# Asking for the first four weight tiles two at a time, and releasing the stores of projections two scores earlier, in an fp32 transformer block on one core

## The chip, the core and the metric

The kernel runs on one core of a Trainium2 chip. The metric is the device time of one execution in microseconds (us); lower is better. The times are medians of several runs. One further execution was recorded by the hardware profiler, and all rows of profiles come from such recorded executions.

The engines are named as in the profile: PE is TensorE (PEld its weight loads), DVE is VectorE, ACT is ScalarE, POOL is GpSimd, and SP is SyncE, which here does nothing but issue DMAs. Each engine works through its own queue in order.

## What is computed

One transformer block with adaptive layer norm on a sequence of 2048 rows of width 512, in float32, with 32 heads of width 16 and a hidden width of 1792:

```python
mod = (_silu(c) @ w_mod).reshape(c.shape[0], 6, 1, -1)
sa, ca, ga, sb, cb, gb = (mod[:, i] for i in range(6))
h = _layernorm(x) * (1 + ca) + sa
x = x + ga * attention(h, wqkv, wo)        # softmax over all 2048 keys, 32 heads
h = _layernorm(x) * (1 + cb) + sb
x = x + gb * (gelu(h @ w1 + b1) @ w2 + b2)
```

## The kernel before

**Precision.** Projections and the two feed-forward products are made of three products each: every operand is split into a high and a low part ("hi" and "lo", or the two halves of a `[P, 2, D]` tile), and high x high, low x high and high x low are added up in one PSUM bank. So each product of a 512-wide contraction is a group of 4 x 3 = 12 matmuls, and one over six hidden blocks of 128 a group of 18.

**Attention sets the pace.** There are 32 units, each with four heads and one batch of 512 queries (four batches `b`, eight units each). A unit has 16 steps, one for each 128 keys. A *half-step* (`half_step`, line 1007) is one such step; there are 512. It makes four *scores* (`exp_mm`, line 626: a matmul "e", then an exponential on ACT), four matmuls "mx" for the row maxima of a later unit (each reduced on DVE), and eight "pv" entries on PE in the profile, the four products of probabilities and values (`pv_step`). Scores and maxima use 64 of the 128 rows of the array, and so a matmul on the other 64 rows can run beside each of them.

**Background work** fills those other rows. `half_step` takes groups from the generator `jobs` (line 959, `work`) and issues up to `RUN` = 6 half-row matmuls of the current group in each half-step (`bg_mm`, line 985), on alternating halves of the rows; a group of 12 thus takes 24 half-row matmuls, four half-steps. When the generator gives `None`, the half-step has no background work and its scores and maxima run beside each other instead. When the two halves follow each other, line 996 makes the first matmul of the new half wait for an ACT instruction noted by `saw` after the last one. Background work is, in order:

- `block0` (line 930): the rest of the projections to queries, keys and values. A group for queries or keys ends in `evac` of `proj_qk` (line 305): ACT copies the bank, POOL makes the high and low part (lines 309, 310), and a store to DRAM is put off by `soon` (line 257). `soon(n, f)` emits `f` once n more scores have been emitted, and counts it in `owed` until then. `store_qk` (line 293) then puts two DMAs on SP.
- At its end, `block0` waits for all that is owed (line 952: no preparation, no owed store, no values and no division under way), closes the memory pools of the projections and opens that of the feed-forward part in the same place (`open_ffn`, line 680).
- For each batch b: `front(b)` (line 803), the output projection with `wo`, the second layer norm and its transposes; then `feed(b)` (line 857), the feed-forward part in three parts. `front` waits until the attention output of its batch is divided (`done[b]`, all four pieces of it), four scores more, and until its four tiles of `wo` have been asked for. `front(b + 1)` stands ahead of the last part of `feed(b)`. In the loop, GELU is done on ACT and POOL: the first half (lines 876 to 879) at the group's end, the second half (lines 882 to 887), which begins with a tanh, ten scores later.

The division (`o_prep`, line 702) reads the attention output of two units back from DRAM, inverts the denominators (14 scores later), stores them (2 later), loads them broadcast (5 later) and divides on POOL (7 later). At most two run at a time; the last one of a batch can begin eight scores after the batch's last unit has ended, and none of batch b begins before the hidden products of batch b - 1 are all emitted (`free_pc`, line 912).

**Weights of the later stages** are split once, kept in DRAM, and come back as tiles of 512 KB in a fixed order (`stream`, line 757: four tiles of `wo`, then those of w1 and w2). `wload` (line 769) asks for the next one if the pool is open and there is room: eight buffers, each free once the tile eight places before has been dropped. `wt` has every tile that was asked for so far, `used` every one that was dropped. Before the change `half_step` calls `wload` at the start of every odd half-step, and of an even one while fewer than `KC` = 4 tiles are waiting to be used.

**Order on the queues** is that of the program's text; there is no scheduler. SP runs ahead of the other engines and stops only where a DMA must wait for data or memory. `step_start` (line 1065) emits at the start of a half-step the loads that are due by then: queries (`qst`) and keys (`kh`) of the unit after next, and values (`vg`) of the next. The row maxima of a unit go through POOL (line 408) and DRAM into `qst` (line 419, "qst<-m") before its first score.

**The tail.** After 512 half-steps a group that is not finished is finished by itself, the last pv between its two halves of rows; then the remaining groups run on all 128 rows, then batch 3's output projection and feed-forward part.

Of the kernel before, what the change touches and what calls it, by code (L numbers as in the profile page):

```python
# [23 lines left out]
KC = D // P  # L24
# [45 lines left out]
def block_kernel(ctx: ExitStack, tc: tile.TileContext, x, wqkv, wo, w1, b1, w2, b2, c, w_mod, out):  # L70
# [88 lines left out]
    def stage(name):  # L159
        if first[0] and name in FIRST:  # L160
            return vpool.tile([P, D], F32, tag=name, name=name, bufs=FIRST[name])
        return spool.tile([P, D], F32, tag=name, name=name, bufs=STAGE[name])

    def pieces(name, dt=FR):
        return spool.tile([P, 2, D], dt, tag="parts", name=name, bufs=3)
# [83 lines left out]
    def later(n, f):  # L249
        if n:  # L250
            hooks.setdefault(clock["t"] + n, []).append(f)
        else:
            f()
# [3 lines left out]
    def soon(n, f):  # L257

        owed[0] += 1

        def g():
            owed[0] -= 1
            f()

        later(n, g)
# [27 lines left out]
    def store_qk(w, k, b, parts):  # L293
        stored.add((w, k, b))
        planes = qk_d[w][k].rearrange("i d o t -> (d o) i t")[:, :, b * TB : (b + 1) * TB]
        sy.dma_start(planes[:, 1 - w : 3 - w], parts.bitcast(F32))
        sy.dma_start(planes[:, 2 * w], parts[:, 0].bitcast(F32))

    def proj_terms(w, k, b):
        hi, lo = hT[b]  # L300
        t = wt_of[w, k]
        n = range(KC)
        return terms3([t[:, 0, i] for i in n], [t[:, 1, i] for i in n], [hi[:, i] for i in n], [lo[:, i] for i in n])

    def proj_qk(w, k, b):
        def evac(ps):
            parts, r = pieces("parts"), stage("pf")
            ac.activation(r, ps, AF.Copy)
            gp.tensor_copy(parts[:, 0], r)
            gp.tensor_tensor(parts[:, 1], r, parts[:, 0].bitcast(F32), op=ALU.subtract)  # L310
            soon(8, lambda: store_qk(w, k, b, parts))

        return proj_terms(w, k, b), "bg", evac

# [62 lines left out]
    def mx_mm(a):  # L377

        u, i = xorder[xc[a]] if xc[a] < 64 else divmod(xc[a], 32)
        xc[a] += 1  # L380
        kr, p, qc = i // 8, (i // 4) % 2, i % 4
        if u not in mxp:
            mxp[u] = small.tile([P, 16, 4], F32, tag="mxp", name="mxp")
            red[u] = 0
        ps = take("mx")
        r0 = a * 64
        te.matmul(ps, qst[u][r0 : r0 + KR, p, qc * P : (qc + 1) * P],  # L387
                  kh(u, kr // 2)[r0 : r0 + KR, p, (kr % 2) * TB : (kr % 2 + 1) * TB], start=True, stop=True)
        hc = (a * 2 + p) * 4 + qc

        def reduce():
            ins = ve.tensor_reduce(mxp[u][:, hc, kr : kr + 1], ps, axis=AX.X, op=ALU.max, negate=True)  # L392
            red[u] += 1
            if red[u] == 64:
                max_rows(u)
            return ins

        return reduce
# [227 lines left out]
    def exp_mm(a, bk="e"):  # L626

        s, p = divmod(ec[a], 2)
        while begun[0] < min(ec) // 2 + 1:
            begun[0] += 1  # L630
            step_start(begun[0] - 1)
        ec[a] += 1
        u, kc = divmod(s, NKC)
        assert u in mrows, (u, ec, xc, red, clock["t"])
        r0 = a * 64
        ps = take(bk)
        te.matmul(ps, kh(u, kc // 8)[r0 : r0 + KX, p, (kc % 8) * P : (kc % 8 + 1) * P], qst[u][r0 : r0 + KX, p],  # L637
                  start=True, stop=True)

        def act():  # L640
            t = ppool.tile([P, TB], F32, tag="p", name="p")
            saw(ac.activation(t, ps, AF.Exp, scale=SCALE))  # L642
            pt[4 * s + p * 2 + a] = t
            advance()

        return act
# [13 lines left out]
    def pv_step():  # L660
        s = cur["pv"]
        cur["pv"] += 1
        u, kc = divmod(s, NKC)
        if kc == 0:
            cur["ps"] = take("pv")
        for j in range(4):
            te.matmul(cur["ps"][32 * j : 32 * (j + 1)], vg[u][:, kc, j * VW : j * VW + 32], pt.pop(4 * s + j),  # L667
                      start=kc == 0, stop=kc == NKC - 1)
        if kc == NKC - 1:
            vg.pop(u)  # L670
            attn_out(u, cur["ps"])


    pools = {}
# [92 lines left out]
    wt, used, ringed, extra = {}, set(), [], []  # L767

    def wload():

        n = len(wt)
        if n == len(stream) or "f" not in pools:
            return
        key = stream[n]
        if extra:
            t = extra.pop()
        elif len(ringed) < WB or ringed[-WB] in used:
            t = pools["f"].tile([P, 2, D], FR, tag="w", name=f"w{key[1]}", bufs=WB)
            ringed.append(key)
        else:  # L780
            return
        sy.dma_start(t.bitcast(F32), {"o": wo_d, 1: w1_d, 2: w2_d}[key[1]][key[2]])
        wt[key] = t
# [201 lines left out]
    def bg_mm(h):  # L985

        g = act["g"]
        terms, bk, evac = g["group"]
        i = g["at"][h]
        if i == len(terms):  # L990
            return False
        if g["n"] == 0:
            g["ps"] = take(bk)
        ins = mm(g["ps"], terms[i], g["n"], 2 * len(terms), slice(h * 64, h * 64 + 64)).ins
        if g["n"] and g["half"] != h:
            tc.add_manual_dep(ins, g["seen"].name, AFTER, reason="both halves of the rows add to one bank")
        g["half"], g["seen"] = h, None
        g["at"][h] += 1
        g["n"] += 1
        if g["n"] == 2 * len(terms):  # L1000
            evac(g["ps"])
            act["g"] = None
        return act["g"] is not None
# [2 lines left out]

    def half_step(hs):
        h = hs % 2
        if h or len(wt) < len(used) + KC:
            wload()  # L1010
        if sides:
            sides.pop(0)()
        full = False
        if act["g"] is None:
            j = held.pop() if held else next(jobs, None)
            if callable(j):
                j()
                full = True
                j = next(jobs, None)
            if callable(j):  # L1020
                held.append(j)
            elif j is not None:
                act["g"] = {"group": j, "at": [0, 0], "n": 0, "seen": None}
        nx = min(64 * NU, LEAD + 4 * (hs + 1))
        ne = 4 * (hs + 1)

        def x_ok(a):
            return sum(xc) < nx and xc[a] < 32 * NU

        def e_ok(a):  # L1030
            return sum(ec) < ne and ec[a] < 2 * NU * NKC

        more = act["g"] is not None
        free = not more and not full
        k = 0
        while more and k < RUN:
            a = 1 - h
            more = bg_mm(h)
            if e_ok(a) and (sum(ec) < ne - 1 and k % 2 == 1 or not x_ok(a) and (sum(ec) < ne - 1 or k == RUN - 1)):
                exp_mm(a)()  # L1040
            elif x_ok(a):
                mx_mm(a)()
            k += 1
        while sum(ec) < ne or sum(xc) < nx:
            a = 0 if ec[0] <= ec[1] else 1
            fs = []
            if sum(ec) < ne:
                fs.append(exp_mm(a, "bg" if free and sum(ec) == ne - 1 else "e"))
                if x_ok(1 - a):
                    fs.append(mx_mm(1 - a))  # L1050
                elif e_ok(1 - a):
                    fs.append(exp_mm(1 - a))
            else:
                fs += [mx_mm(i) for i in range(2) if x_ok(i)]
            for f in fs:
                f()
        if hs:
            assert min(ec) >= 2 * cur["pv"] + 2
            pv_step()
# [24 lines left out]
    for hs in range(NU * NKC):  # L1084
        half_step(hs)
# [137 lines left out]
```

## Time and profile before

| | us |
|---|---|
| median of 3 runs | 1738.71 (1736.97 to 1739.3) |
| the profiled execution | 1738.16 |
| its span, from its first instruction to its last | 1736.3 |
| busy: PE, DVE, ACT, POOL | 1710.8, 1375.2, 1241.8, 685.0 |
| mean granted clock of TensorE | 0.997 |

In the profile's rows a DMA has the name of what it writes and what it reads (`wo<-wos`), and L782 is line 782 of the kernel. A row of the timeline or of the chain has the start in us, the length in us, the engine, and how many instructions of a kind were joined (x8). A row of waits names who waited for whom, the total in us, how often, and the longest. The stretches give for each of PE, PEld, DVE, ACT and POOL the busy time in us and the count of instructions, then the granted clock of TensorE, the share of the DMA engines, and GB/s.

### The profile page before, as it was taken

Reading aid. Unit: us, or ns where it says so; the run is one execution under the profiler, and the core shown is the slowest. Engines: PE = TensorE matmul, PEld = TensorE weight load, DVE = VectorE, ACT = ScalarE, POOL = GpSimd, SP = SyncE. Lnnn points to the kernel's source line nnn. Section 1 sums busy time; section 2 is a strip of 40 time slices with the busy share of each in tenths; the row PEclk is TensorE's granted clock in tenths of the full one; section 3 lists DMA queues with packets and bytes.
Section 4 is the critical chain, followed back from the end, with each engine's and each line's share of the span. In section 5 each row is a group of like instructions: output and inputs, shape, how many; then the busy total and the mean of one; then the engine's idle time right before and its main releaser. Section 6 shows DMA issues by size and latency. Waiting matters only on the chain.

```text
span 1736.3 us, 32537 instructions
## 1 busy us (share of the span) xinstructions
PE 1710.8 (99%) x12121; PEld 891.1 (51%) x12121; DVE 1375.2 (79%) x2298; ACT 1241.8 (72%) x2379; POOL 685.0 (39%) x688
## 2 busy tenths in 40 slices
PE   7999999999999999999999999999999999999999
PEld 6654444444444444444445444444445444444777
DVE  7998888888888888888889888888888888860332
ACT  3357778778777778778777778777877778778231
POOL 7333434435121256404631356404631356525310
PEclk8999999999999999999999999999999999999999
DMA  8646776767447534335454444335364344323554
GB/s 292 205 142 200 221 218 182 236 179 223 125 136 206 125 86 117 94 85 136 113 168 106 124 114 105 94 81 166 100 174 114 101 132 114 97 66 111 195 156 166
DMA packets 137130, 251.90 MB, mean 145 GB/s; under 512 B 25854, under 2 KB 45324, under 8 KB 136972
## 3 DMA queue, kind: packets, MB, share of 16 engines
q1 hardware_dynamic: 135712, 248.19, 50.3%
q8 instruction: 96, 1.57, 0.4%
q10 hardware_dynamic: 1260, 1.63, 0.3%
q14 instruction: 62, 0.51, 0.1%
HBM read 188.49 MB, written 61.28 MB: 144 GB/s over the span
## 4 chain that ended last, share of the span: by engine, by line
PE 91%; DVE 4%; ACT 2%; POOL 1%; DMA 1%; issue 1%; SPq 0%; ACTq 0%; POOLq 0%; DVEq 0%
PE bg L274 46%; PE pv L667 29%; PE e L637 11%; PE mx L387 3%; DVE mxp L392 2%; ACT p L642 1%; PE pr L274 1%; PE o L274 1%; PE warm L438 1%; DVE hTlo L481 1%; DVE bst L235 0%; ACT h L849 0%; DMA qst<-m 0%; PE mx L333 0%; PE bg L847 0%
## 5 line engine op out<-in xcount | busy, mean ns | idle before, releaser
L392 DVE TENSOR_REDUCE mxp<-mx 128x1 f32<-128x512 f32 x2048 | 1269.4, 682 | 201.4 <-PE mx L387 182.5
L642 ACT ACTIVATE p<-e 128x512 f32<-128x512 f32 x2032 | 1064.4, 605 | 308.1 <-PE e L637 292.8
L387 PE MATMUL mx<-kh,qst 48*128 48x512 f32 x2048 | 873.3, 441 | 1.9 <-DVE mxp L392 0.4
L637 PE MATMUL e<-qst,kh 50*128 50x512 f32 x2032 | 754.6, 419 | 7.0 <-ACT p L642 6.3
L667 PE MATMUL pv<-p,vg 128*32 128x512 f32 x4096 | 546.6, 605 | 0.0
L637 PEld LDWEIGHTS e<-qst,kh 50*128 50x128 f32 x2032 | 373.7, 186 | 148.7 <-ACT p L642 141.8
L387 PEld LDWEIGHTS mx<-kh,qst 48*128 48x128 f32 x2048 | 368.6, 185 | 21.1 <-DVE mxp L392 16.2
L274 PE MATMUL bg<-w,g 64*128 64x512 f32 (+1 forms) x1044 | 277.8, 404 | 0.0
L274 PEld LDWEIGHTS bg<-w,g 64*128 64x128 f32 (+1 forms) x1044 | 183.0, 185 | 142.7 <-ACT p L642 103.3
L274 PE MATMUL bg<-pchi,w 64*128 64x512 f32 (+1 forms) x656 | 194.5, 416 | 2.1 <-ACT p L642 2.0
L274 PEld LDWEIGHTS bg<-pchi,w 64*128 64x128 f32 (+1 forms) x656 | 109.0, 184 | 150.3 <-ACT p L642 102.2
L274 PE MATMUL bg<-hThi,wqkv 64*128 64x512 f32 x560 | 167.4, 418 | 0.3 <-ACT p L642 0.3
L274 PEld LDWEIGHTS bg<-hThi,wqkv 64*128 64x128 f32 x560 | 92.8, 184 | 118.9 <-ACT p L642 106.3
L667 PEld LDWEIGHTS pv<-p,vg 128*32 128x32 f32 x4096 | 81.4, 108 | 125.4 <-issue 117.6
L884 POOL TENSOR_SCALAR s<-s 128x512 f32<-128x512 f32 x40 | 59.8, 1496 | 137.4 <-ACT s L882 127.0
L903 POOL TENSOR_TENSOR x<-y,x 128x512 f32<-128x512 f32 x28 | 35.9, 1281 | 144.3 <-ACT y L902 139.3
L274 PE MATMUL bg<-pclo,w 64*128 64x512 f32 (+1 forms) x328 | 88.6, 389 | 0.0
L872 DVE TENSOR_TENSOR g<-h,g 128x512 fp32r<-128x512 f32 x16 | 11.6, 723 | 91.5 <-PE bg L274 62.7
L274 PE MATMUL bg<-hTlo,wqkv 64*128 64x512 f32 x280 | 76.4, 392 | 0.0
L819 POOL TENSOR_TENSOR x<-y,x 128x512 f32<-128x512 f32 x12 | 15.4, 1282 | 140.9 <-ACT y L816 114.8
L274 PEld LDWEIGHTS bg<-pclo,w 64*128 64x128 f32 (+1 forms) x328 | 60.5, 184 | 12.3
L274 PE MATMUL bg<-wo,pchi 64*128 64x512 f32 x192 | 64.8, 417 | 0.0
(160 smaller groups left out, 1331.9 us busy)
## 6 DMA issues: line engine op xcount, KB each, us to landing
kh<-qk SPq DMA_DIRECT2D x256, 192.0 KB
w<-w1s SPq DMA_DIRECT2D x56, 512.0 KB
w<-w2s SPq DMA_DIRECT2D x53, 512.0 KB
vg<-v SPq DMA_DIRECT2D x64, 332.0 KB
qk<-parts SPq DMA_DIRECT2D x32, 512.0 KB
qst<-qk SPq DMA_DIRECT2D x64, 192.0 KB
qk<-parts SPq DMA_DIRECT2D x32, 256.0 KB
ou<-osb SPq DMA_DIRECT2D x32, 256.0 KB
```

The source lines that it names most:

```text
L274: return te.matmul(ps, term[0][r], term[1][r], start=i == 0, stop=i == n - 1)
L387: te.matmul(ps, qst[u][r0 : r0 + KR, p, qc * P : (qc + 1) * P], kh(u, kr // 2)[r0 : r0 + KR, p, (kr % 2) * TB : (kr % 2 + 1) * TB], start= ...
L392: ins = ve.tensor_reduce(mxp[u][:, hc, kr : kr + 1], ps, axis=AX.X, op=ALU.max, negate=True)
L438: te.matmul(warm[:, :P], ident, ident, start=True, stop=True)
L481: e.tensor_tensor(hT[b][1][:, f], keep.pop(("H", b, f)), hT[b][0][:, f].bitcast(F32), op=ALU.subtract)
L637: te.matmul(ps, kh(u, kc // 8)[r0 : r0 + KX, p, (kc % 8) * P : (kc % 8 + 1) * P], qst[u][r0 : r0 + KX, p], start=True, stop=True)
L642: saw(ac.activation(t, ps, AF.Exp, scale=SCALE))
L667: te.matmul(cur["ps"][32 * j : 32 * (j + 1)], vg[u][:, kc, j * VW : j * VW + 32], pt.pop(4 * s + j), start=kc == 0, stop=kc == NKC - 1)
L819: gp.tensor_tensor(x2[t], y, x2[t], op=ALU.add)
L872: ve.tensor_tensor(g[:, 1], h, g[:, 0].bitcast(F32), op=ALU.subtract)
L884: gp.tensor_scalar(s, s, 1.0, None, op0=ALU.add)
L903: later(4, lambda: gp.tensor_tensor(x2[t], y, x2[t], op=ALU.add))
```

## The change

The store of a projection's parts is emitted six scores after the projection, not eight. And in a half-step, as long as the pool is open and fewer than four tiles have been asked for at all, `wload` is called twice; otherwise the old rule holds.

```diff
@@ -308,7 +308,7 @@
             ac.activation(r, ps, AF.Copy)
             gp.tensor_copy(parts[:, 0], r)
             gp.tensor_tensor(parts[:, 1], r, parts[:, 0].bitcast(F32), op=ALU.subtract)
-            soon(8, lambda: store_qk(w, k, b, parts))
+            soon(6, lambda: store_qk(w, k, b, parts))
 
         return proj_terms(w, k, b), "bg", evac
 
@@ -1006,7 +1006,7 @@
 
     def half_step(hs):
         h = hs % 2
-        if h or len(wt) < len(used) + KC:
+        for _ in range(2 if "f" in pools and len(wt) < KC else h or len(wt) < len(used) + KC):
             wload()
         if sides:
             sides.pop(0)()
```

## The prediction

> **What bounds the kernel now.** I read the page's shares first, then its chain, then the chain in order of time around the place that the change touches.
>
> ```profile
> span 1736.3 us, 32537 instructions
> PE 1710.8 (99%) x12121; PEld 891.1 (51%) x12121; DVE 1375.2 (79%) x2298; ACT 1241.8 (72%) x2379; POOL 685.0 (39%) x688
> PE 91%; DVE 4%; ACT 2%; POOL 1%; DMA 1%; issue 1%; SPq 0%; ACTq 0%; POOLq 0%; DVEq 0%
> ```
>
> TensorE (PE) is busy for 99% of the span and is 91% of the chain. So the change gains only where it puts PE work beside work that has to be done anyway, and loses wherever PE is made to stand. The profiled execution took 1738.16 us: span 1736.30 and 1.86 around it. It lies 0.55 us under the median of the runs, 1738.71.
>
> The chain around the first output projection shows the size of a half-step, which ends with eight "pv" matmuls:
>
> ```profile
> 518.98 1.00 PE pv L667 x8
> ...
> 521.88 1.00 PE pv L667 x8
> ...
> 530.11 1.00 PE pv L667 x8
> 531.10 0.42 PE e L637
> ...
> 538.32 1.00 PE pv L667 x8
> 539.32 0.45 PE bg L274
> ...
> 541.28 1.00 PE pv L667 x8
> ```
>
> From 518.98 to 521.88 is a half-step with background work (bg): 2.90 us; from 538.32 to 541.28 another, 2.96; I take 2.92. Between 521.88 and 538.32 there is no bg: 16.44 us are six idle half-steps of 2.74. I call them I1 to I6; I4 begins at 531.1, after the pv of 530.11. So a half-step's worth of bg, when it is put into an idle half-step, costs only 0.18 us there. Waiting for the four tiles of wo is part of these six.
>
> **What the change does, by the code's own clock.** A half-step is four scores. The last projection's copy (line 308) is emitted at the sixth bg matmul of its half-step, when two scores of it are done. Eight scores later is the middle of I2, so line 952 passes at the start of I3, and the four tiles are asked for at the starts of I4, I5, I6 and the next half-step; the projection begins there, at 539.3. Six scores later is the end of I1: line 952 passes at I2, two tiles are asked for at I3 and two at I4, and the projection begins in I4. Three half-steps earlier, then. `len(wt)` counts all tiles ever asked for, so the rule of two acts at these two half-steps alone.
>
> **Cost 1: do the tiles land in time?** SyncE (SP) runs ahead of PE and stops only at waits. Its queue, the POOL instruction that it waits for, and its longest wait here:
>
> ```profile
> 521.85 0.79 SPq L360 DMA_DIRECT2D kh<-qk  x2
> 524.39 0.38 SPq L296 DMA_DIRECT2D qk<-parts  x1
> 524.82 0.47 SPq L297 DMA_DIRECT2D qk<-parts  x1
> 530.71 0.80 SPq L782 DMA_DIRECT2D wo<-wos  x2
> 531.55 1.88 SPq L801 DMA_DIRECT2D x<-in_A_x_dram  x4
> ```
>
> ```profile
> 523.07 1.29 POOL L310 TENSOR_TENSOR parts<-pf,parts 128x512 fp32r<-128x512 f32 x1
> ```
>
> ```profile
> SPq L782 <- DMA qk<-parts: 5.3, 1, 5.3
> ```
>
> The store already leaves 0.03 us after POOL ends (524.36). Releasing it at six scores cannot send it sooner; SP just stands there earlier. Nor is the first wo load held by its place in the program: it waits 5.3 us for the stores to land, because it reuses their memory, and goes at 530.71, 0.4 us before I4 begins. So the tiles are needed earlier than the DMA can bring them. One thing helps: the pair of kh loads (2 x 192 KB) is emitted at the start of I2, after the end of I1, so it now comes behind the store. How fast the data move:
>
> ```profile
> 529.00:530.00 1.00, 0.90 (x6) 0.25 (x2) 1.00 (x2) 1.00 (x3) 0.00 (x0) 1.00 0.35 131
> 530.00:531.00 1.00, 1.00 (x9) 0.16 (x8) 1.00 (x3) 0.89 (x2) 0.00 (x0) 1.00 0.01 2
> 531.00:532.00 1.00, 1.00 (x11) 0.69 (x7) 0.74 (x2) 0.44 (x1) 0.00 (x0) 1.00 0.35 49
> 532.00:533.00 1.00, 0.88 (x7) 0.34 (x9) 1.00 (x3) 1.00 (x3) 0.00 (x0) 1.00 0.60 225
> 533.00:534.00 1.00, 1.00 (x10) 0.23 (x4) 1.00 (x2) 0.63 (x2) 0.00 (x0) 1.00 1.04 426
> 534.00:535.00 1.00, 0.96 (x7) 0.46 (x5) 0.74 (x3) 0.70 (x2) 0.00 (x0) 1.00 0.98 393
> ```
>
> The last column is GB/s, so kB in each microsecond. A tile is 512 KB, 524 kB. From 531 the sum is 49, 274, 700, 1093 kB: the first tile's data are through at 533.6, the second's at 534.9. The stores' data ended by 530.0 and SP was released at 530.7, so I add 0.7 for the signal: 534.3 and 535.6, or 3.6 and 4.9 us after the first issue. The kh pair's 393 kB, at the 294 kB per us that the four busy rows average, are 1.3 us of queue that no longer stand ahead of the stores: first issue 529.4, tiles usable at 533.0 and 534.3 (estimates).
>
> PE gets to the first bg matmul of I4 at 531.1 and stands until 533.0: **1.9 us**. The next three terms need tile 0 alone; with their partners they take 3 x 0.23 us, so PE asks for tile 1 at 533.7 and stands another **0.6 us**. Tiles 2 and 3 are needed two half-steps later, over 5.8 us on, and follow the others at 1.3 us each; no wait. Sum +2.5 us, all of it on the path, since PE has no slack in a bg half-step. Bounds: if the moved kh loads help nothing, 3.2 + 0.6 = 3.8; if the stores land 2 us sooner still, 0.6 is left.
>
> **Cost 2: what the earlier start is worth.** Of the three half-steps one is lost at the next batch. Batch 1's projection waits for `done[1]`, whose last part starts eight scores after attention unit 15 ends, a fixed half-step, and takes 14+2+5+7 = 28 scores (lines 702 to 739). By these counts it is complete just before bg arrives there now; with bg three half-steps early, it comes one half-step sooner than now (its second-last part no longer holds it), and the projection starts two sooner. The third idle half-step simply moves there. At batch 2 the chain moves along with bg. So two idle half-steps fill: 2 x 0.18 = **+0.36 us** in the loop, and at the loop's end half a group (12 of 24 half-row matmuls) more is done. The tail:
>
> ```profile
> 1611.61 2.67 PE pv L667 x16
> 1614.28 19.32 PE bg L274 x84
> ```
>
> Now exactly seven whole groups of 12 follow: 19.32 / 84 = 0.23 us each, 2.76 a group. Afterwards six groups follow, but the loop leaves a half-finished one, whose other 12 half-row matmuls run alone, first six of one half, then the last pv, then six of the other. A half-row matmul alone isn't in the trace; between 0.115 (as in a pair) and 0.23 I take 0.23, since the chain gives that for each one with its partner beside it: 12 x 0.23 = 2.76, no gain (at the other end, -1.4). And the second half must wait for the copy of pv (line 996's dependency on `seen`), 0.60 us and a signal: **+0.75 us**.
>
> ```profile
> 1614.32 0.60 ACT L654 ACTIVATE osb<-pv 128x512 f32<-128x512 f32 x1 [1.15 <-PE pv L667]
> ```
>
> **Gain: two stalls that depend on where bg stands.** One is in the chain before unit 16:
>
> ```profile
> 848.84 1.28 POOL g L887
> 850.12 0.17 POOL m L408
> ...
> 856.16 7.22 DMA qst<-m
> ```
>
> ```profile
> PEld e L637 <- DMA qst<-m: 1.0, 1, 1.0
> ```
>
> The row maxima queue on POOL behind a GELU's second half and their load then arrives 1.0 us late. Three half-steps earlier that GELU is out of the way: **-1.0 us**. The other is near the loop's end, where a tanh stands behind POOL's division for batch 3; two half-steps earlier the tanh comes ahead of it: **-0.4 us**.
>
> ```profile
> ACT s L882 <- POOL s L879: 0.4, 1, 0.4
> ```
>
> The other stores move too, but only the kh pair of each unit's 13th step and an occasional preparation load come behind them, and those are read several half-steps later: nothing.
>
> **Sum:** 2.5 + 0.36 + 0.75 - 1.0 - 0.4 = +2.2 us, 1738.16 to 1740.4; on the median of the runs, 1740.9 (0.13% more). A measurement of this kernel can tell about 0.2%, 3.5 us, from no change, so I forecast no difference by that bound, on the slow side.
>
> **Rivals.**
> (a) *The stand of PE trips its clock* (slower). Near the start:
>
> ```profile
> 31.00:35.00 4.00, 1.63 (x12) 1.39 (x12) 3.93 (x9) 2.96 (x5) 3.73 (x7) 0.96 0.79 291
> 35.00:39.00 4.00, 3.41 (x15) 2.41 (x14) 4.00 (x5) 3.11 (x6) 3.60 (x4) 0.50 0.65 214
> 39.00:43.00 4.00, 2.87 (x10) 2.11 (x9) 3.93 (x7) 0.30 (x1) 3.46 (x4) 0.50 1.01 213
> 43.00:47.00 4.00, 4.00 (x15) 3.21 (x14) 3.97 (x6) 0.60 (x1) 3.09 (x3) 0.76 0.63 138
> ```
>
> After 4 us in which PE was busy for 1.63, the granted clock was 0.50 for some 10 us (0.3 by the 0.96 of the first row, 8, and 1.9 by the 0.76 of the last). Half-steps are bound by PE, so 10 us at half clock lose 5: 2.2 + 5 = +7.2 us, 1745.9 on the median. For it: 1.9 + 0.6 us of standing within 3.2 us leaves PE as little busy as there. Against: it is in two pieces, and has to fall right in whatever stretch the clock looks at. It decides from about 2 us of standing within one such stretch. Chance 0.13. The Trainium skill, "TensorE: Matmul & The Clock Gate", section "What's actually happening", says that the clock falls to half after at least one idle window of about 3.4 us; by that rule, read strictly, PE's 2.5 us in two pieces would trip nothing, while the rows show a drop where PE was still 41% busy.
>
> (b) *The stall of unit 16 moves instead of going* (slower). Two half-steps earlier, the GELUs of batches 1 and 2 stand to the row maxima as those of batch 0 do now. If three or four of the later units then pay 1.0 us each and that of unit 16 stays, 2.2 + 1.0 + 3.5 = +6.7, 1745.4 on the median. Against: that wait is the only one of its kind in the whole span, though every GELU stretch of batch 0 has this order, and division loads stood beside it on SP. Chance 0.13.
>
> (c) *The tiles come in time* (nearly nothing): stall 0.6 and drained matmuls at the pair's price, 0.6 + 0.36 + 0.75 - 1.4 - 1.4 = -1.1, 1737.6. Chance 0.14. The plan as its words put it, three half-steps of bg hidden and no stall, would be worth 3 x (6 x 0.115 - 0.18) = 1.5 us; with both stalls gone and no wait in the tail, -2.9 us, 1735.8. A faster result beyond 0.2% needs a further stall to vanish that I don't see: 0.06.
>
> **How the numbers follow.** My case 0.54, (a) 0.13, (b) 0.13, (c) 0.14, faster 0.06. My case with the stall's bounds spans 1739 to 1742.2 (1738.71 plus 0.3 to 3.5), with little of it past +3.5 us. The range takes in (c) and most of (a) and (b): 1736.8 to 1746.5. Faster 0.06; same 0.67 (0.53 of my case and all of (c)); slower 0.27.
>
> **What would show it.** The first bg matmul with wo three half-steps after the last projection instead of six; idle of PE before it, ended by the wo load, of about 1.9 us (3.2 at most), then a smaller one; four wo loads in a row on SP right after the stores land, and the kh pair behind the stores. Three idle half-steps ahead of batch 1's projection in place of two. No wait for qst<-m ahead of unit 16. In the tail 72 whole matmuls, not 84. Wrong would be: a first load still at 530.7 (stall 3.8), a granted clock of 0.5 after 531, or new waits for qst<-m in batches 1 and 2.

## The result, and the profile after

The changed kernel takes 1733.8 us (median of 11 runs, 1733.15 to 1734.94) against 1738.52 us before (11 runs, 1736.7 to 1739.3): a ratio of 0.9975, 95% interval 0.9966 to 0.9984. It is faster by 0.25%, 4.7 us; the forecast was 2.2 us slower, and the range did not reach that far. The profiled execution took 1734.07 us. The page of the changed kernel (span, busy time, chain by engine):

```profile
span 1732.3 us, 32497 instructions
PE 1702.9 (98%) x12133; PEld 893.2 (52%) x12133; DVE 1374.4 (79%) x2297; ACT 1246.5 (72%) x2379; POOL 693.3 (40%) x695
PE 91%; DVE 3%; ACT 2%; DMA 2%; POOL 1%; issue 1%; SPq 0%; ACTq 0%; POOLq 0%; DVEq 0%
```

The shares have hardly moved: a page like this can't show where 4 us went. The course of the kernel does. The "pv" matmuls come eight to a half-step (4096 for 512), so their starts give the start of every half-step. After minus before, in us:

| at half-step | 128 | 144 | 496 | 511 | end of the span |
|---|---|---|---|---|---|
| after minus before | -1.06 | +4.19 | -4.07 | -2.53 | -4.06 |

The -1.06 stands there before the two programs differ; most of it (-0.97) already at half-step 0, where the profiles of the twelve further kernels lie from 0.57 us earlier to 1.39 later than the kernel before. I count it as the spread of single executions. Then come a loss of 5.25 us in half-steps 128 to 144, a gain of 8.26 in the loop, and a tail that comes out even.

**The loss** is where the forecast looked for one. SyncE's queue in the changed kernel:

```profile
523.26 0.39 SPq L296 DMA_DIRECT2D qk<-parts  x1
523.69 1.38 SPq L297 DMA_DIRECT2D qk<-parts  x1
525.17 0.90 SPq L360 DMA_DIRECT2D kh<-qk  x2
528.22 1.76 SPq L782 DMA_DIRECT2D wo<-wos  x4
```

The kh pair now stands behind the stores, and four loads of wo go in a row. The chain of waits in order of time, and its pv rows:

```profile
526.25 1.00 PE pv L667 x8
...
528.22 3.52 DMA wo<-wos
531.74 0.24 issue
...
535.34 1.86 PE pv L667 x8
...
539.60 1.00 PE pv L667 x8
...
542.52 0.99 PE pv L667 x8
```

The first tile is usable 3.5 us after its issue, and the row of waits `PE bg L274 <- DMA wo<-wos` gives PE's stand:

```profile
PE bg L274 <- DMA wo<-wos: 2.0, 1, 2.0
```

The pv at 535.34 took 1.86 us, not 1.00. Stretches (columns as before; the granted clock follows POOL's busy time):

```profile
528.13:531.54 3.41, 1.75 (x12) 0.34 (x9) 2.10 (x4) 1.65 (x4) 0.00 (x0) 1.00 0.71 219
535.00:538.40 3.40, 3.40 (x16) 1.28 (x16) 1.31 (x3) 1.09 (x2) 0.00 (x0) 0.50 1.06 404
538.40:542.00 3.60, 3.60 (x30) 1.84 (x28) 3.07 (x6) 3.35 (x7) 0.00 (x0) 1.00 0.14 53
```

After 3.41 us in which PE was busy for 1.75, the clock records show 0.50 from 531.54 for 6.83 us. So rival (a) of the prediction came true, on top of the stall.

**The gain** is spread over the loop and has no wait of its own in the list of waits. It shows when the exponentials of ScalarE are read half-step by half-step. First the timeline of ACT in the kernel before (start, length, the number of exponentials in a row, and the idle time ahead of them):

```profile
1082.08 2.07 ACT L642 ACTIVATE p<-e 128x512 f32<-128x512 f32 x4 [0.28 <-PE e L637]
1085.00 2.06 ACT L642 ACTIVATE p<-e 128x512 f32<-128x512 f32 x4 [0.85 <-PE e L637]
...
1087.91 2.06 ACT L642 ACTIVATE p<-e 128x512 f32<-128x512 f32 x4 [0.34 <-PE e L637]
1090.83 1.09 ACT L642 ACTIVATE p<-e 128x512 f32<-128x512 f32 x2 [0.85 <-PE e L637]
```

and the same view of the changed kernel:

```profile
1078.73 2.07 ACT L642 ACTIVATE p<-e 128x512 f32<-128x512 f32 x4 [0.30 <-PE e L637]
1081.58 1.13 ACT L642 ACTIVATE p<-e 128x512 f32<-128x512 f32 x2 [0.79 <-PE e L637]
...
1084.49 2.07 ACT L642 ACTIVATE p<-e 128x512 f32<-128x512 f32 x4 [0.22 <-PE e L637]
1087.35 2.11 ACT L642 ACTIVATE p<-e 128x512 f32<-128x512 f32 x4 [0.79 <-PE e L637]
...
1090.26 2.07 ACT L642 ACTIVATE p<-e 128x512 f32<-128x512 f32 x4 [0.29 <-PE e L637]
1093.11 1.13 ACT L642 ACTIVATE p<-e 128x512 f32<-128x512 f32 x2 [0.78 <-PE e L637]
```

Before, the first exponentials follow each other at 2.92 and 2.91 us, each time. After, the steps are 2.85, 2.91, 2.86, 2.91, 2.85: every other half-step is 0.06 us shorter. The idle time ahead has two sizes (0.8 or 0.3, by whether another ACT instruction stands between), and the longer one is 0.06 less where the step is shorter (0.79 for 0.85). The chain's pv rows of the changed kernel have the same rhythm, and the pair of "e" ahead of each pv is where it is lost:

```profile
1079.53 0.35 PE e L637 x2
1079.88 0.99 PE pv L667 x8
...
1082.46 0.27 PE e L637 x2
1082.73 1.00 PE pv L667 x8
...
1085.31 0.33 PE e L637 x2
1085.65 1.00 PE pv L667 x8
...
1088.23 0.26 PE e L637 x2
1088.49 1.00 PE pv L667 x8
```

What differs is a wait. An exponential writes one of ten p buffers. Some exponentials have two waits, one for PE's score and one for ScalarE's own count (the number of instructions that it has finished), which stands for an earlier user of that buffer. The own count is that of an exponential six to ten places earlier (of the 645 such waits of the kernel before, 372 are ten, 235 eight places), so on an engine that works in order it is always met; but two waits take an instruction more: an EVENT_SEMAPHORE waits for the score, and the exponential behind it for the own count. The exponentials' line (L642) between 1076 and 1092, kernel before:

```profile
L642 ACT ACTIVATE p<-e x22: 592/599/622, 1076.3 to 1091.3; 128x512 f32<-128x512 f32 x22
L642 ACTq EVENT_SEMAPHORE  x8: 17/17/17, 1076.2 to 1090.8; - x8
```

and after:

```profile
L642 ACT ACTIVATE p<-e x24: 591/600/617, 1075.8 to 1091.7; 128x512 f32<-128x512 f32 x24
L642 ACTq EVENT_SEMAPHORE  x6: 17/17/17, 1076.3 to 1090.2; - x6
```

Where such an instruction stands decides. In the kernel before, the *first* exponential of every half-step has one. ScalarE is waiting for a score there. In half-steps 176 to 264 that score's matmul ends 1.73 us after the half-step's first pv, with the extra instruction or without it; the exponential starts 0.100 us later with it (at 1.83) and 0.038 without (at 1.77). The trace shows the extra instruction's start 0.062 ahead of the exponential's, so it stands where the exponential would have started, and the delay arises on ScalarE, not in the score. The fourth score of the half-step takes the PSUM bank that it frees (its weight load goes at 2.48, not 2.42), and the next pv follows that score. In the changed kernel, from the first output projection on, the wait stands in every other half-step on the *second* exponential. That one starts 0.04 us later for it (2.305 us after the pv, against 2.265 in run 7 below, which has no extra wait there), but no half-step is longer: 2.853 us with it, 2.852 without any. In half-steps 176 to 264, before has the wait on 89 first exponentials, median length 2.916 us; after has 44 with it (2.911) and 45 without (2.853). A half-step thus costs **0.058 us** more with the wait on its first exponential. In half-steps 144 to 495 the kernel before has 328 of them and the changed one 169: 159 x 0.058 = 9.2 us.

### The profile page after: what moved, and what is told of

It reads as the page before. It is cut to its first block, busy times and chain, and to the rows that moved or that the text cites. A ratio compares the mean times of both kernels' runs of the same rounds, so it can differ in the third digit from the quotient of the medians.

```text
span 1732.3 us, 32497 instructions
## 1 busy us (share of the span) xinstructions
PE 1702.9 (98%) x12133; PEld 893.2 (52%) x12133; DVE 1374.4 (79%) x2297; ACT 1246.5 (72%) x2379; POOL 693.3 (40%) x695
## 4 chain that ended last, share of the span: by engine, by line
PE 91%; DVE 3%; ACT 2%; DMA 2%; POOL 1%; issue 1%; SPq 0%; ACTq 0%; POOLq 0%; DVEq 0%
PE bg L274 46%; PE pv L667 29%; PE e L637 10%; PE mx L387 3%; DVE mxp L392 2%; ACT p L642 1%; PE pr L274 1%; PE o L274 1%; PE warm L438 1%; DMA wt<-wos 0%; ACT h L849 0%; PE mx L333 0%; DVE bst L235 0%; PE bg L847 0%; DMA qst<-qk 0%
## 5 line engine op out<-in xcount | busy, mean ns | idle before, releaser
L642 ACT ACTIVATE p<-e 128x512 f32<-128x512 f32 x2035 | 1073.1, 604 | 300.0 <-PE e L637 292.9
L274 PE MATMUL bg<-w,g 64*128 64x512 f32 (+1 forms) x1056 | 280.4, 404 | 0.0
L274 PEld LDWEIGHTS bg<-w,g 64*128 64x128 f32 (+1 forms) x1056 | 185.3, 185 | 143.0 <-ACT p L642 83.9
L274 PE MATMUL bg<-pchi,w 64*128 64x512 f32 (+1 forms) x664 | 197.5, 417 | 2.3 <-ACT p L642 2.2
L274 PEld LDWEIGHTS bg<-pchi,w 64*128 64x128 f32 (+1 forms) x664 | 110.1, 184 | 153.2 <-ACT p L642 103.4
L274 PE MATMUL bg<-hThi,wqkv 64*128 64x512 f32 x560 | 167.4, 418 | 0.3 <-ACT p L642 0.3
L274 PEld LDWEIGHTS bg<-hThi,wqkv 64*128 64x128 f32 x560 | 92.7, 184 | 118.9 <-ACT p L642 106.3
L274 PE MATMUL bg<-pclo,w 64*128 64x512 f32 (+1 forms) x332 | 90.2, 391 | 0.0
L903 POOL TENSOR_TENSOR x<-y,x 128x512 f32<-128x512 f32 x28 | 36.0, 1286 | 132.9 <-ACT y L902 132.9
L274 PE MATMUL bg<-hTlo,wqkv 64*128 64x512 f32 x280 | 76.3, 391 | 0.0
L274 PE MATMUL bg<-wo,pchi 64*128 64x512 f32 x192 | 66.1, 424 | 2.0 <-DMA wo<-wos 2.0
L274 PEld LDWEIGHTS bg<-pclo,w 64*128 64x128 f32 (+1 forms) x332 | 61.2, 184 | 12.2
L408 POOL CAST m<-mt 128x32 fp32r<-128x32 f32 x32 | 6.8, 212 | 147.8 <-DVE mt L406 147.8
```

The source lines that it names most:

```text
L274: return te.matmul(ps, term[0][r], term[1][r], start=i == 0, stop=i == n - 1)
L408: gp.tensor_copy(m2[:, 0], mt)
L903: later(4, lambda: gp.tensor_tensor(x2[t], y, x2[t], op=ALU.add))
```

## The experiments

**R (rhythm)** is this theory: the gain is the extra wait off the first exponential in every other half-step. Which exponential gets it depends on how the order of taking and freeing p buffers is shifted; with this ring, an even number of idle half-steps ahead of the first output projection (six before) leaves it on every first one, an odd number (three after) on every other. **W**: the gain is background work that starts earlier. **B**: the buffers themselves, how many are free and where they lie. The table has all runs: first exponentials with the wait in half-steps 144 to 495 (counted in the order of the program), what these half-steps took against the kernel before (profiled executions), the median, and the ratio of the times to before in the same session.

| run | waiting firsts | loop, us | median us | ratio, 95% interval |
|---|---|---|---|---|
| before | 328 | 0 | 1738.52 | 1 |
| after | 169 | -8.26 | 1733.8 | 0.9975 (0.9966 to 0.9984) |
| stores at six alone | 169 | -8.39 | 1736.62 | 0.9987 (0.9978 to 0.9996) |
| two tiles alone | 330 | -0.42 | 1741.97 | 1.0019 (1.0010 to 1.0027) |
| before, one idle half-step more | 168 | -8.96 | 1732.82 | 0.9968 (0.9957 to 0.9980) |
| after, one idle half-step more | 330 | -0.92 | 1740.54 | 1.0014 (1.0005 to 1.0023) |
| nine p buffers | 169 | -8.94 | 1725.12 | 0.9921 (0.9908 to 0.9935) |
| idle half-step at the start | 168 | -9.65 | 1729.29 | 0.9948 (0.9934 to 0.9961) |
| eight p buffers | 328 | -0.86 | 1737.51 | 0.9995 (0.9986 to 1.0003) |
| two rings, idle at the start | 11 | -18.35 | 1716.66 | 0.9876 (0.9862 to 0.9889) |
| seven p buffers | 10 | +10.59 | 1756.61 | 1.0104 (1.0090 to 1.0118) |
| after with nine p buffers | 174 | -6.75 | 1732.86 | 0.9969 (0.9956 to 0.9981) |
| two rings, idle, and the change | 162 | -10.13 | 1728.95 | 0.9946 (0.9933 to 0.9958) |
| after with two rings | 11 | -17.32 | 1721.67 | 0.9905 (0.9890 to 0.9920) |

Without the row of seven buffers, a straight line through the loop column has 0.054 us per waiting first exponential, and no row lies 2 us or more off it.

**1. Stores at six alone.**

```diff
-            soon(8, lambda: store_qk(w, k, b, parts))
+            soon(6, lambda: store_qk(w, k, b, parts))
```

> The stores at six scores alone; weight tiles still one per step. Theory R (rhythm): the first output projection starts one half-step earlier than before, after an odd number (5) of idle half-steps, and from there on every other half-step has its extra wait (reuse of a p buffer) on the second exponential, not the first: about 155 half-steps at 0.058 us less, -9 us, and no stand of PE of 2 us ahead of it, so no fall of the clock: about 1729 us, faster than both kernels. Rival W (the gain is background work that starts earlier): one half-step earlier is a third of the whole change, so 1735 to 1738 us.

Measured 1736.62 us, the number that W expected. But half-steps 144 to 496 gained 8.39 us, as R has it, and half-steps 128 to 144 lost only 0.17: no stand. The end gave 6.4 back, 2.2 in the last 15 half-steps and 4.3 behind them. The first rows of the tail after the loop's leftover groups, timeline of PE in this kernel:

```profile
1628.23 0.94 PE L274 MATMUL bg<-wt,g 128*128 128x512 f32 x3 [2.68 <-DMA wt<-w2s]
1629.51 1.23 PE L274 MATMUL bg<-wt,g 128*128 128x512 f32 x3 [0.34 <-DMA wt<-w2s]
```

PE outruns the weight stream, and the stand halves the clock for 3.41 us from 1629.98. R's mechanism held; its total of 1729 did not, since the tail wasn't in it.

**2. Two tiles per step alone** (line 1009, without the other).

```diff
-        if h or len(wt) < len(used) + KC:
+        for _ in range(2 if "f" in pools and len(wt) < KC else h or len(wt) < len(used) + KC):
```

> Two weight tiles per step alone; stores still at eight scores. The first output projection starts two half-steps earlier than before, after an even number (4) of idle half-steps. Theory R: the extra wait stays on the first exponential of every half-step as before, no gain: 1738 to 1740 us (a short stand of PE for the tiles possible). Rival W: two thirds of the earlier start, so 1733 to 1735.5 us.

Measured 1741.97, slower than before; the loop is unchanged (-0.42), as R expects. The two microseconds above R's range are a stand of 0.7 us (below, timeline of PE) and 2.6 us in the tail. The clock did not fall here.

```profile
534.80 0.46 PE L274 MATMUL bg<-wo,pchi 64*128 64x512 f32 x1 [0.71 <-DMA wo<-wos]
```

**3. The kernel before with one idle half-step more**, at line 810 in `front`:

```diff
+        for _ in range(1 if b == 0 else 0):
+            yield None
```

> The kernel before with one more idle half-step ahead of the first output projection: seven, an odd number. It does nothing of the change and starts the background work later. Theory R: every other half-step loses the extra wait on its first exponential: about -9 us, 1729 to 1731 us. Rival W: later is worse or nothing, 1738.5 to 1741.5 us.

Measured 1732.82 us. Nothing of the change, background work *later*, and the kernel is as fast as the changed one, with -8.96 us in the loop. It is 1.8 us past R's range; the tail gives 3.2 back. That excludes W as the cause of the loop's gain.

**4. The changed kernel with the same two lines added.**

> The changed kernel with one more idle half-step ahead of the first output projection: four, an even number, so that the tiles also have one half-step more to land. Theory R: the gain is gone though both edits are in and the stall of 2 us is gone too: 1737 to 1739 us. Rival W: without the stall the change is better than ever, 1728 to 1733 us.

Measured 1740.54: both edits in, no stand and no half clock (half-steps 128 to 144 lose 0.36 us), and the gain is gone (1.5 us past R's range, with 3.2 lost behind half-step 496). What is left of the loop's gain, 0.92 us, lies in half-steps 240 to 256 (-1.03): it is the stall ahead of unit 16 that the prediction priced at 1.0.

**5. Nine p buffers**, nothing of the change:

```diff
-    ppcm, ppool = pool("p", bufs=10)
+    ppcm, ppool = pool("p", bufs=9)
```

> The kernel before with 9 p buffers in the place of 10, nothing of the change. By building, the half-steps whose first exponential carries the extra wait fall from 477 to 235. Theory R: 242 x 0.058 = -14 us, 1722 to 1728 us (the tail may move by a few us either way with the phase; up to half-step 496 -12 to -15). Rival B (the wait is paid because p buffers come free late): one buffer fewer is slower or the same, 1738 to 1745 us.

Measured 1725.12, as R expects; one buffer *less* gains 0.8%.

**6. One idle half-step at the start** (`yield None` as the first line of `block0`).

> The kernel before with one idle half-step ahead of its first block of background work, nothing of the change. 235 half-steps with the wait on the first exponential in place of 477. Theory R: -14 us, 1722 to 1728 us, half of it (-4) already in half-steps 0 to 135. Rival W (the gain of the change is background work that starts earlier): everything starts one half-step later, 1738 to 1740 us.

Measured 1729.29, 1.3 us past R's range; up to half-step 496 the gain is 12.4 us, and the tail gives back 3.5. By half-step 128 it is 2.6, not the 4 expected.

**7. Two rings of five p buffers, with the idle half-step of run 6.**

```diff
-            t = ppool.tile([P, TB], F32, tag="p", name="p")
+            t = ppool.tile([P, TB], F32, tag=f"p{p}", name="p", bufs=5)
```

> The idle half-step of the run before this, and the ten p buffers as two rings of five, one for each row half, so that almost no exponential carries the extra wait any more (27 first exponentials in place of 477). Theory R: 450 x 0.058 = -26 us, 1710 to 1716 us, half-steps with background work at 2.85 us throughout. Rival B: ten buffers as before, so nothing beyond the noise; or the limit of a half-step moves to another engine and the gain stops at that of every other half-step, 1722 to 1728 us.

The rings go by `p`, which tells the two heads of a row half apart; the edit does not make one ring for each row half, as the expectation has it. Measured 1716.66, ratio 0.9876: it beats both kernels, by 22 and 17 us, and lies 0.7 past R's range. R's 26 us are there up to half-step 496 (-25.58), and the tail takes 3.4 back. The timeline of ACT has the short step throughout:

```profile
1087.81 1.09 ACT L642 ACTIVATE p<-e 128x512 f32<-128x512 f32 x2 [0.79 <-PE e L637]
...
1090.66 2.07 ACT L642 ACTIVATE p<-e 128x512 f32<-128x512 f32 x4 [0.21 <-PE e L637]
1093.51 2.07 ACT L642 ACTIVATE p<-e 128x512 f32<-128x512 f32 x4 [0.78 <-PE e L637]
```

1087.81, 1090.66, 1093.51: 2.85 us each. Between 1076 and 1092, line L642 has no EVENT_SEMAPHORE at all in this kernel.

**8. Seven p buffers** (`bufs=7`).

> The kernel before with 7 p buffers. By building only 10 half-steps keep the extra wait on the first exponential; it stands on the second and the fourth instead. Theory R: if only the first counts, -27 us, 1709 to 1716 us. If a wait on the fourth counts as well (it is the last of the half-step and its bank is taken again next), no gain or a loss. Rival B: three buffers fewer are slower, 1740 us and more.

Measured 1756.61: slower, where R's first number was 1709 to 1716. Most half-steps in the loop do take 2.85 us (median 2.854 in half-steps 176 to 264), though nearly all have the wait on their fourth exponential. So a wait there need not lengthen a half-step. But 20 of these 89 take 3.20 to 3.23: with seven buffers the exponentials wait for real, for the pv that reads the buffer. From the list of waits (total, times, longest); the kernel before has no such row:

```profile
ACT p L642 <- PE pv L667: 254.3, 409, 1.1
```

**9. Eight p buffers** (`bufs=8`).

> The kernel before with 8 p buffers: by building the same number of half-steps as before (478) carries the extra wait on the first exponential. Theory R: no gain from a smaller ring as such, 1737 to 1740 us, half-steps at 2.91 us throughout (unless a p buffer is truly late, as with seven). Rival: the gain of the ring of nine came from another place or spacing of the buffers, so a ring of eight gains as well, 1725 to 1732 us.

Measured 1737.51, the same as before: the interval includes 1. So the size of the ring does nothing by itself; nine differs from eight and ten in where it puts the wait.

**10. The changed kernel with nine p buffers.**

> The changed kernel with 9 p buffers. With nine, the change leaves the number of waiting first exponentials in the loop as it is (166 with and without it; 22 in place of 3 at the end). Theory R: against nine buffers without the change (0.9921 of before) the change then shows its other costs alone, the stand of 2 us, the half clock and a filled idle part, +3 to +7 us: 1728 to 1732 us with before at 1738.5. Rival W: the change brings its 4.7 us here too, 1719 to 1722 us.

Measured 1732.86: in a kernel in which it leaves the rhythm alone, the same change costs 1732.86 - 1725.12 = 7.7 us. That is a little over R's range. The two profiles differ by 6.6: 4.1 in half-steps 128 to 144 (a stand of 2.09 us, then half clock for 3.41), 2.2 in the loop, 1.2 at the end, and -0.9 ahead of half-step 128. The 2.2 I can't name.

**11. The change on top of run 7.**

> The change on top of the two rings of five with the idle half-step at the start. By building, it brings the wait back to 160 first exponentials in the loop, where 6 were. Theory R: 160 x 0.058 = 9 us and the stand with its half clock, 5 us: the same change makes this kernel 10 to 14 us slower, 1727 to 1731 us against 1716.7. Rival W: the change is worth what it is worth in the first kernel, 1712 us.

Measured 1728.95 against 1716.66: the change that makes the first kernel 4.7 us faster makes this one 12.3 slower. It brings 151 waiting first exponentials back (+8.2 us in the loop), and PE stands for 2.99 us ahead of a half clock of 6.83.

**12. The changed kernel with the two rings of five**, without the idle half-step.

> The changed kernel with the two rings of five and no idle half-step: 67 waiting first exponentials in half-steps 0 to 135, 5 in the rest of the loop, 21 at the end, 93 in place of 300. Theory R: 207 x 0.058 = -12 us against the changed kernel, 1720 to 1724 us. Rival B (the buffers themselves): the same ten buffers, so no change, 1733 to 1734 us.

Measured 1721.67, 12.1 us less than the changed kernel, as R expects.

## Why the prediction was wrong, step by step

- **The step that failed** is in rival (c): "A faster result beyond 0.2% needs a further stall to vanish that I don't see". What vanished was too small to be seen as a stall: 0.058 us in every other half-step of the loop. Behind it stands "I take 2.92": I took the length of a half-step with background work as a constant. It is 2.853 us where the first exponential has one wait, and 2.91 where it has two. The missing term: half-steps 144 to 496 gained 8.26 us, and only 1.0 of it is the unit 16 of the sum. (159 x 0.058 and unit 16 would be 10.2; I can't name the 1.9 between.) A PE that is busy for 99% hid it, since a busy PE row only says that some matmul is under way.
- **Stall for the tiles:** forecast 1.9 + 0.6, measured 2.0. First issue to usable tile: forecast 3.6 us, measured 3.52. Tile 1's stand of 0.6 did not appear; PE was at half clock by then.
- **The filled idle half-steps** (cost 2): the step "The third idle half-step simply moves there" failed too. Counted by their bg matmuls, two half-steps without background work stand ahead of batch 1's projection (263 and 264), as before (266 and 267), not three. All background work stays three half-steps early to the end of the loop, so three are filled, not two: 3 x 0.18 = 0.54 us for 0.36. Run 4, which fills two, lost 0.36 in half-steps 128 to 144, as the prediction priced it.
- **Rival (a)** had the right place and point ("from about 2 us of standing") and too large a price: half-steps 128 to 144 lost 5.25 in all, 2.0 of it the stall. With 0.54 for the three filled half-steps, 2.7 are left for the clock, against 5. It fell for 6.83 us, not for ten.
- **Unit 16:** forecast -1.0, and run 4, in which the rhythm is as before, shows -1.03 there. The row `qst<-m` of the list of waits is gone: the stall did not move elsewhere, and rival (b) did not happen. The row is gone in run 3 as well, whose background work stands one half-step later.
- **The tanh wait** was forecast to go (-0.4). The row of waits grew from 0.4 to 0.7.
- **Tail:** forecast +0.75, the wait for the copy of pv between the two halves of a half-finished group. That wait is not in the changed kernel: with all three half-steps kept, the group has only six half-row matmuls left, and they fit ahead of the last pv (timeline of PE):

```profile
1608.36 0.74 PE L274 MATMUL bg<-pchi,w 64*128 64x512 f32 x2
1608.94 1.09 PE L274 MATMUL bg<-pclo,w 64*128 64x512 f32 x4
1609.96 1.06 PE L667 MATMUL pv<-p,vg 128*32 128x512 f32 x8
```

In run 2, which starts two half-steps early, 12 are left and the wait is there, as forecast:

```profile
1616.82 0.73 PE L274 MATMUL bg<-pchi,w 64*128 64x512 f32 x2 [0.72 <-ACT osb L654]
```

The changed kernel lost 1.54 in half-steps 496 to 511 and gained about the same behind them, in sum nothing. Behind them it has 72 whole matmuls, not 84, as forecast (2.76 us less), against waits of 1.2 us that the sum did not have, for batch 3's tiles of wo:

```profile
1628.14 0.97 PE L274 MATMUL o<-wt,kh 128*128 128x512 f32 x3 [0.54 <-DMA wt<-wos]
1629.43 0.97 PE L274 MATMUL o<-wt,kh 128*128 128x512 f32 x3 [0.32 <-DMA wt<-wos]
1630.72 9.81 PE L274 MATMUL o<-wt,kh 128*128 128x512 f32 x42 [0.32 <-DMA wt<-wos]
```

Together, for the profiled executions: +5.25 in half-steps 128 to 144 (2.0, 0.54 and 2.7), -8.26 in the loop, nothing in the tail, and -1.06 ahead of all this, that is -4.1 us. Stall and half clock made the change slower, as feared, and the rhythm, which the change does not aim at, paid for them. The gain is luck, not what the change was made for: runs 4, 10 and 11 have the same change without it. Could it have been read beforehand? Not by comparison: in half-steps 176 to 264 the kernel before has none without the wait on its first exponential. But the instruction itself, 0.062 us ahead of its exponential, was there, on the exponentials' line over the whole span of the kernel before (length: lowest, median, highest in ns):

```profile
L642 ACTq EVENT_SEMAPHORE  x646: 17/17/2329, 106.2 to 1610.9; - x162
```

Open: how the bookkeeping of buffers turns one idle half-step into another place of the wait I only counted, not derived; and why the exponential follows an instruction of 17 ns only 62 ns after its start.

## What to carry to other kernels

When a loop is bound by a chain through several engines, compare the length of one iteration in the two kernels before looking for big waits: 0.058 us in every other of some 350 iterations outweighed every stall that could be named. Look for waits that are always met, too: here an instruction with a second wait started 0.04 to 0.06 us later, and that lengthened the loop only where the next step of the chain hung on this instruction. And a change that only shifts the phase of a loop can gain or lose by that alone; shift it by one step without the change before crediting the change.

## What the runs showed of the hardware

- In single profiled executions, a stand of PE of 2 us was enough to halve the granted clock, but not for a fixed time: 1.93 us and 2.09 us gave 3.41 us at half clock (runs 12 and 10), 2.00 and 2.99 gave 6.83 (after, run 11), 2.68 in run 1's tail 3.41; 0.71 us (run 2) and 1.56 (run 3's tail) gave none. The Trainium skill, "TensorE: Matmul & The Clock Gate", section "What's actually happening", has a free-running window of 3413 ns, and lengths of 3.41 and 6.83 agree with it. Its "after ≥1 idle window" does not: the clock fell at the end of 3.41 us in which PE was busy for 1.75. The busy share alone does not decide it either: near the start of the changed kernel, 3.41 us with PE busy for 1.66 (from 29.78) were followed by no fall.
- A wait that is already met is not free on ScalarE: the instruction shows 17 ns, but the exponential starts 0.062 us after that instruction's start, which is 0.058 us on the chain of a half-step. On a second exponential the delay was 0.04 us, and the half-step was no longer for it.
